# A linear-attention and bilinear-FFN block: the second layer norm of chunks 3 and 4 regrouped through DRAM and transposed in 32x32 blocks

## The chip, the cores and the metric

The kernel runs on one core of one Trainium2 chip. The core has five engines that run their own instruction streams and meet at semaphores: TensorE (PE; its weight loads are listed apart as PEld), VectorE (DVE), ScalarE (ACT), GpSimd (POOL) and SyncE (SP), which here only issues DMAs. The metric is the device time of one execution in microseconds, lower is better; a time shown is the median of several runs.

## What is computed

A transformer block with adaptive layer norm on 2048 tokens of width D = 512: attention without softmax with 32 heads, then a gated FFN of width F = 1376 without a nonlinearity. Everything is float32.

```
mod = (silu(c) @ w_mod).reshape(1, 6, 1, 512)
sa, ca, ga, sb, cb, gb = mod[:, 0] ... mod[:, 5]
h = layernorm(x) * (1 + ca) + sa
x = x + ga * linear_attention(h, wqkv, wo)
h = layernorm(x) * (1 + cb) + sb          # the second layer norm
x = x + gb * (((h @ w_gate) * (h @ w_up)) @ w_down)
```

## The kernel before

**Tiling.** The 2048 tokens are four chunks of four tiles; a tile is 128 tokens (partitions) by 512. The code counts chunks from 0, so "chunks 3 and 4" of the change are `ch` = 2 and 3. Each f32 product is made of three products in a narrower float format: an operand is split into a rounded high part and the rest (`split`, L190: high on ACT at L191, low on DVE or POOL at L192), and high x high, high x low, low x high are summed in PSUM.

**Buffers.** Nearly all tiles come from one pool `tiles` of NB = 99 buffers of 2 KB a partition (L62, `B` L75). PSUM is two pools of four banks, `ps_acc` and `ps_w`. The schedule is manual: each engine executes its instructions in the order in which the Python code issues them. A buffer is handed on when its last reader is done; an engine that writes into it waits for that. All DMAs go through SP's queue in program order.

**The second layer norm** (`Norm`, L212). Per chunk: statistics on DVE; `rstd_of` and `nmr_of`; `xhat(j)` (L238) normalises tile j on ACT, or `xhat_on` (L244) on DVE; `transpose(k)` (L250) turns feature block k (128 features) of the four tiles by four TensorE transposes of 128x128 into one PSUM bank of 128 features x 512 tokens; `modulated` (L263) applies scale `cb[k]` and shift `sb[k]` on ACT from PSUM into an SBUF tile `f` and stores it to DRAM (`kept`). `ln2_turn` (L803) does both for some k. Chunks 0 and 1 (`PLAIN`) are split into high and low there too. Chunks 2 and 3 are loaded back from `kept` later, by `Left.get`.

**The FFN by blocks.** The chunks are taken in pairs, (0, 1) then (2, 3). For one pair and one F tile the gate and up products are made with seven matrix products instead of eight: `Left` (L819) builds from the four quarters a11, a12, a21, a22 of the transposed activations the sums s1 to s4 (DVE) and splits them; `Right` (L874) does the same with the rows of w_gate and w_up (differences on POOL at L888, splits at L899 to L906). For k = 0, 1 (`KH` = 2), a11 is feature block k of the first chunk and a12 block k + 2; a21 and a22 are those of the second chunk. `block` (L938) makes the seven products of one F tile, six matmuls each (`times`, L915), in the banks a, b, c, d:

```
g1: a  = a11 x b11      ACT: copy a to b        p1
g2: d  = s1 x t1        ACT: copy d to u        p5
g3: b += s2 x t2        ACT: copy b to c, to u2 p6
g4: a += a12 x b21                              p2
g5: c += s3 x t3        DVE: p5 = c + u (L979)  p7
g6: d += s4 x b22       DVE: u2 = d + u2 (L983), times a (L948)  p3
g7: c += a22 x t4       DVE: times c (L948)     p4
```

ACT's copies are L925 (called from L956, L962, L966, L968). PE may start g5 only when ACT has copied b to c, and g7 only when DVE has read c at L979. p1 to p7 are points at which other work is put into the engines' streams: p6 scales the w_down tile (L1071), p7 loads the next w_down tile and the weights of block m + 2 and splits those of m + 1, p3 splits the w_down tile, p4 makes the sums of m + 2. At p1, before it, `flush` issues the splits (`kh`, `kl`) of the block before.

**Order around the change.** `ffn` (L1058) is a generator over the blocks m = 0, 1, ... of `steps`; `fill(n)` advances it by n products. The main program (L1105 on) weaves attention of the last chunk, layer norm and FFN together by hand. For `ch` = 2, `ln2_turn` stands beside the attention output of tiles 12 and 13 (L1208, L1212; its PE neighbours are `turn_a` L654, `y_step` L690 and `down` L791). For `ch` = 3 it stands within blocks m = 1 and 2 (L1246 to L1258); there the transposes write to `ps_acc` banks. Then the Left side of the second pair is a list `trickle` of small work items (sums and splits); `some` hands out one at each of the points p1, p5, p6, p3, p4 of blocks m = 2 to 6 (L1077: in m = 2 only at the last three). The split parts go to DRAM (`aside`) and are fetched at blocks 7 and 8. After the first pair's second group, matmuls of the down projection (L1000 to L1002) stand between blocks.

Of the kernel before, what the change touches and what calls it, by code (L numbers as in the profile page):

```python
# [8 lines left out]
F32 = mybir.dt.float32  # L9
F32R = mybir.dt.float32r  # L10
AF = mybir.ActivationFunctionType
# [1 line left out]
AX = mybir.AxisListType  # L13

P = 128
NB = 99
EPS_LN = 1e-5
EPS_PHI = 1e-6
EPS_DEN = 1e-6
# [3 lines left out]
def tile_adaln_block(  # L23
# [12 lines left out]
    nc = tc.nc  # L36
    ctx.enter_context(tc.manual_schedule())
    _, S, D = x.shape
    F = w_gate.shape[1]
    KD = D // P  # L40
    NJ = 4
    CH = NJ * P
    NCH = S // CH
# [10 lines left out]
    wo_v = wo.rearrange("(k p) n -> k p n", p=P)  # L54
    wg_v = w_gate.rearrange("(k p) f -> p k f", p=P)
    wu_v = w_up.rearrange("(k p) f -> p k f", p=P)
    wm_v = w_mod.rearrange("(p k) n -> p k n", k=KD)

    pool = lambda name, bufs, **kw: ctx.enter_context(tc.tile_pool(name=name, bufs=bufs, **kw))
    consts = pool("consts", 1)  # L60
    small = pool("small", 2)
    tiles = pool("tiles", NB)  # L62
    ps_acc = pool("ps_acc", 4, space=bass.MemoryType.PSUM)
# [11 lines left out]
    def B(tag, shape=(P, D), dt=F32):  # L75

        return T(tiles, tag, shape, dt)
# [23 lines left out]
    nc.gpsimd.memset(eps_phi, EPS_PHI)  # L101
    eps_z = consts.tile([P, 1], F32, name="eps_z")
    nc.gpsimd.memset(eps_z, S * EPS_PHI)
    half = consts.tile([P, NJ], F32, name="half")
    nc.gpsimd.memset(half, -0.5)


    def load(src, tag):
        raw = B(tag, (P, *src.shape[1:]))[:src.shape[0]]
        nc.sync.dma_start(raw, src)  # L110
        return raw
# [371 lines left out]
    for i in range(NT):  # L483
        ch, j = divmod(i, NJ)
# [59 lines left out]
    ga, sb, cb = rows[2], cols[3], cols[4]  # L544
# [61 lines left out]
    for k in range(KD):  # L606
        f = B("n")
# [10 lines left out]
    for g in range(KD):  # L618
        a, b = g * P, (g + 1) * P
# [30 lines left out]
    def turn_a(i):  # L650
        tps[i] = turn_bank[0]()
        phi = phq.pop(i)
        for k in range(KD):
            nc.tensor.transpose(tps[i][:, k * P:(k + 1) * P], phi[:, k * P:(k + 1) * P], ident)  # L654
# [64 lines left out]
    norm2 = {}  # L719


    PLAIN = (0, 1)
# [73 lines left out]
    def ln2_xhat(ch):  # L796
        norm2[ch].xhat(0, 1, 2, 3)

    def ln2_nx(ch):
        norm2[ch].nmr_of()  # L800
        ln2_xhat(ch)

    def ln2_turn(ch, *ks, cast=None):  # L803
        norm2[ch].transpose(*ks)
        norm2[ch].modulated(cb, sb, *ks, keep=kept[ch], cast=cast, parts=ch in PLAIN)

    for f in lone:
        load_ffn(f)
    kept = [[tc.dram_tile([P, D], F32, name=f"kept_{ch}_{k}") for k in range(KD)] for ch in range(NCH)]
    for ch in range(NCH):  # L810
        norm2[ch] = Norm(xts[ch])

# [3 lines left out]
    KH = KD // 2  # L816
    SIDE = ("a11", "s1", "s2", "a12", "s3", "a22", "s4")

    class Left:  # L819
# [7 lines left out]
        def get(self, *names):  # L827
            for n in names:
                c, k = self.of[n]
                self.f[n] = load(kept[c][k], "f")  # L830

        def sum(self, *names):
            for n in names:
# [40 lines left out]
    class Right:  # L874


        def __init__(self, f):
            f0, self.n = fts[f]
            self.up, self.low = self.tile("raw"), self.tile("raw")
            for t, kh in ((self.up, 0), (self.low, 1)):  # L880
                for i, v in enumerate((wg_v, wu_v)):
                    nc.sync.dma_start(t[:, i], v[:, kh * KH:(kh + 1) * KH, f0:f0 + self.n])

        def tile(self, tag, dt=F32):
# [139 lines left out]
    steps = [(cs, f) for cs, g in groups for f in g]  # L1024
    rights = {}

    def right_load(n):
        if n < len(steps):
            rights[n] = Right(steps[n][1])

    def right_sums(n, on=None):
        if n < len(steps):
# [14 lines left out]
    trickle = []  # L1047
# [10 lines left out]
    def ffn():  # L1058

        first_side, second_side = side, {}  # L1060
        m = 0
        for g, (cs, fs) in enumerate(groups):
            last = g + 1 == len(groups) or groups[g + 1][0] != cs
            outs, ds = [], []
            A = first_side if cs == (0, 1) else second_side
            for f in fs:
                out = []
                draw = draws.pop(m)

                def scale(d=draw):  # L1070
                    nc.vector.tensor_tensor(d, d, gb[:d.shape[0]], op=ALU.mult)  # L1071

                at = {"p6": [scale],
                      "p7": [lambda: draw_load(m + 1), lambda: right_load(m + 2), lambda: right_split(m + 1)],
                      "p3": [lambda: ds.append(split_raw(draw, low=nc.gpsimd))],
                      "p4": [lambda: right_sums(m + 2)]}
                for point in ("p1", "p5", "p6", "p3", "p4")[2 if m == 2 else 0:]:  # L1077
                    at.setdefault(point, []).append(lambda: some(some_at.get(m, 0)))
                if m + 1 < len(steps) and steps[m + 1][0] != cs:
                    at["p1"].append(lambda: fetch(stash, second_side, "a11", "s1"))  # L1080
                    at["p7"].insert(0, lambda: fetch(stash, second_side, "s2", "a12", "s3"))
# [12 lines left out]
            parts.extend([(ch, i, js, outs, ds, last) for i, (ch, js) in enumerate(zip(cs, jss)) if js] for jss in cut_at)  # L1094
        flush()
        while parts:
            group = parts.pop(0)
            for p in group:
                down_group(*p, by_tile=not parts, end=not parts and p is group[-1])()

    def fill(n):
        for _ in range(n):
            next(work, None)
# [93 lines left out]
    first[0].sum("s1", "s3")  # L1197
    g()
    norm2[2].xhat(2, 3)
    turn_a(12)  # L1200
    take = down(1, (0, 1), parts=((f0, f1), (f2,)))
    turn_h(12)
# [2 lines left out]
    y_banks += [acc_bank(), acc_bank()]  # L1205
    y_seed(12, y_bank)
    first[0].sum("s2", "s4")
    ln2_turn(2, 0, 1)  # L1208
    take()
    den_c(14)  # L1210
    y_step(12, seed=y_bank)
    ln2_turn(2, 2, 3)  # L1212
    take = down(1, (2, 3))
    first[1].sum("s1", "s3", "s2", "s4")
    first[0].split("s1", "s2")
# [26 lines left out]
    norm2[3].rstd_of()  # L1242
    fill(3)
    norm2[3].nmr_of()
    fill(1)
    norm2[3].xhat(0)  # L1246
    norm2[3].xhat_on(nc.vector, 2)
    second = [Left((2, 3), k).aside(stash) for k in range(KH)]
    for x in second:
        x.get("a11", "a12")  # L1250
    fill(2)
    norm2[3].xhat(1)
    fill(1)
    norm2[3].xhat(3)
    fill(2)
    ln2_turn(3, 0, 1)
    fill(1)
    ln2_turn(3, 2, 3)  # L1258
    for x in second:
        x.get("a21", "a22")  # L1260
    for part in zip(*[x.steps() for x in second]):
        for todo_k in part:
            trickle += todo_k
    free[0] = True
    for _ in work:
        pass
# [27 lines left out]
```

## Time and profile before

| | |
|---|---|
| median of 3 runs | 564.64 us (564.09 to 564.94) |
| the profiled execution | 563.91 us |
| its span in the trace | 562.2 us |
| mean granted TensorE clock | 0.999 of full speed |
| PE, DVE, ACT, POOL busy | 556.0, 379.3, 280.7, 192.4 us |
| DMA | 59.34 MB, 106 GB/s on average |

The profile is that of one execution. A line of the timeline gives start and duration in us, engine, source line, operation, output <- inputs with their shape, and how many instructions in a row were joined (x8); in brackets stands the idle time before it and what released it. The duration of a joined row is from the first start to the last end; an instruction's duration contains a part that overlaps the next one's, so the spacing of starts is the pace. A line of a group gives "busy us, mean ns of one | idle before, and who released". A DMA issue line gives count, KB each and the median time from issue to landing. The row of a window gives start:end and its length, then the busy time of PE, PEld, DVE, ACT and POOL with instruction counts, the granted clock, the DMA share and GB/s.

### The profile page before, as it was taken

What the parts mean: (1) busy time and instruction counts of PE and PEld (TensorE: products, weight loads), DVE (VectorE), ACT (ScalarE), POOL (GpSimd) and SP (SyncE); (2) the same over time, 40 slices, a digit from 0 to 9 for tenths busy, and PEclk for the clock granted to TensorE, in tenths of its full rate; (3) what the DMA queues carried; (4) which work ended last, traced back from release to release, by engine and by line L of the source; (5) the groups of instructions that cost most, each with busy time, mean ns of one, the idle gap of its engine ahead of it and who ended that gap; (6) DMA issues with size and microseconds to landing.
All of it is one profiled execution on the core that took longest, in us unless ns stands there. A gap on an engine that the chain in (4) does not pass through costs nothing.

```text
span 562.2 us, 7362 instructions
## 1 busy us (share of the span) xinstructions
PE 556.0 (99%) x2565; PEld 456.9 (81%) x2565; DVE 379.3 (67%) x622; ACT 280.7 (50%) x503; POOL 192.4 (34%) x195
## 2 busy tenths in 40 slices
PE   8999999999999999999999999999999999999997
PEld 6788888888888788878888888887888888888886
DVE  7896968878969876769887877655444444334435
ACT  3695866546557537355885454534333333334120
POOL 2000000000011300001499856556667446446200
PEclk9999999999999999999999999999999999999999
DMA  8900223302302001804409372699337022100004
GB/s 271 386 17 2 75 76 102 124 0 63 93 2 75 1 1 56 244 0 151 132 1 301 111 231 88 202 356 288 113 112 199 7 58 58 56 19 2 0 1 149
DMA packets 50309, 59.34 MB, mean 106 GB/s; under 512 B 6432, under 2 KB 27168, under 8 KB 50272
## 3 DMA queue, kind: packets, MB, share of 16 engines
q1 hardware_dynamic: 50272, 58.87, 32.7%
q8 instruction: 20, 0.33, 0.2%
q14 instruction: 17, 0.14, 0.1%
HBM read 43.12 MB, written 15.73 MB: 105 GB/s over the span
## 4 chain that ended last, share of the span: by engine, by line
PE 92%; issue 2%; POOL 2%; DVE 1%; ACT 1%; DMA 1%; SPq 1%; POOLq 0%
PE bank L920 29%; PE acc L1000 6%; PE acc L1001 6%; PE acc L1002 6%; PE acc L690 6%; PE bank L204 5%; PE bank L206 5%; PE bank L205 5%; PE acc L333 3%; PE acc L332 3%; PE acc L331 3%; PE bank L769 2%; PE bank L767 2%; PE bank L768 2%; PE bank L254 2%
## 5 line engine op out<-in xcount | busy, mean ns | idle before, releaser
L920 PE MATMUL bank<-h,w 128*128 128x512 f32 (+1 forms) x798 | 184.7, 390 | 0.0
L920 PEld LDWEIGHTS bank<-h,w 128*128 128x128 f32 (+1 forms) x798 | 148.3, 186 | 32.7 <-DVE u L979 0.3
L925 ACT ACTIVATE bank<-bank 128x512 f32<-128x512 f32 (+1 forms) x38 | 22.1, 583 | 143.1 <-PE bank L920 143.1
L754 DVE TENSOR_TENSOR x<-acc,x 128x512 f32<-128x512 f32 (+1 forms) x73 | 48.9, 682 | 47.7 <-PE acc L1002 46.9
L906 POOL TENSOR_TENSOR w<-raw,w 128x256 fp32r<-128x256 f32 (+3 forms) x38 | 41.9, 1103 | 101.9 <-ACT w L899 74.7
L1000 PE MATMUL acc<-w,kh 128*128 128x512 f32 (+2 forms) x154 | 59.6, 387 | 0.0
L1001 PE MATMUL acc<-w,kh 128*128 128x512 f32 (+2 forms) x154 | 59.6, 387 | 0.0
L1002 PE MATMUL acc<-w,kl 128*128 128x512 f32 (+2 forms) x154 | 59.5, 386 | 0.0
L192 POOL TENSOR_TENSOR w<-raw,w 128x512 fp32r<-128x512 f32 (+1 forms) x25 | 35.4, 1419 | 54.2 <-ACT w L191 28.4
L232 POOL TENSOR_TENSOR rstd<-ve,half 128x4 f32<-128x4 f32 (+1 forms) x10 | 10.7, 1068 | 122.7 <-DVE ve L231 121.7
L906 POOL TENSOR_TENSOR w<-t,w 128x512 fp32r<-128x512 f32 (+1 forms) x38 | 49.3, 1315 | 0.0
L192 DVE TENSOR_TENSOR kl<-u,kh 128x512 fp32r<-128x512 f32 (+1 forms) x38 | 27.6, 767 | 31.5 <-ACT kh L191 25.8
L204 PE MATMUL bank<-w,h 128*128 128x512 f32 x104 | 40.8, 392 | 0.0
L206 PE MATMUL bank<-w,h 128*128 128x512 f32 x104 | 40.5, 390 | 0.0
L205 PE MATMUL bank<-w,h 128*128 128x512 f32 x104 | 40.5, 389 | 0.0
L690 PE MATMUL acc<-w,xh 128*128 128x512 f32 x120 | 38.1, 399 | 0.0
L1000 PEld LDWEIGHTS acc<-w,kh 128*128 128x128 f32 (+1 forms) x154 | 28.9, 188 | 6.0
L1002 PEld LDWEIGHTS acc<-w,kl 128*128 128x128 f32 (+1 forms) x154 | 28.9, 188 | 6.0
L1001 PEld LDWEIGHTS acc<-w,kh 128*128 128x128 f32 (+1 forms) x154 | 28.9, 188 | 5.9
L979 DVE TENSOR_TENSOR u<-bank,u 128x512 f32<-128x512 f32 (+1 forms) x19 | 13.1, 691 | 29.4 <-PE bank L920 25.9
L241 ACT ACTIVATE n<-x,nmr,rstd 128x512 f32<-128x512 f32 x29 | 22.1, 803 | 16.1 <-DVE nmr L235 14.8
L191 ACT ACTIVATE w<-raw 128x512 fp32r<-128x512 f32 (+2 forms) x44 | 26.4, 619 | 3.0 <-DMA raw<-in_A_wqkv_dram 1.3
(199 smaller groups left out, 1116.0 us busy)
## 6 DMA issues: line engine op xcount, KB each, us to landing
raw<-in_w_mod_dram SPq DMA_DIRECT2D x24, 256.0 KB, 4.6
raw<-in_B_w_down_dram SPq DMA_DIRECT2D x20, 256.0 KB, 3.2
raw<-in_B_w_gate_dram SPq DMA_DIRECT2D x36, 128.0 KB, 3.6
raw<-in_B_w_up_dram SPq DMA_DIRECT2D x36, 128.0 KB, 3.6
x<-in_A_x_dram SPq DMA_DIRECT2D x16, 256.0 KB, 5.4
kept<-f SPq DMA_DIRECT2D x16, 256.0 KB, 2.0
f<-kept SPq DMA_DIRECT2D x16, 256.0 KB, 4.6
side_s<-h SPq DMA_DIRECT2D x16, 256.0 KB, 2.4
```

The source lines that it names most:

```text
L191: nc.scalar.activation(h, src, AF.Copy)
L192: (low or nc.vector).tensor_tensor(l, src, f32(h), op=ALU.subtract)
L204: nc.tensor.matmul(ps, ah, bh, start=i == 0, stop=False)
L205: nc.tensor.matmul(ps, ah, bl, start=False, stop=False)
L206: nc.tensor.matmul(ps, al, bh, start=False, stop=i == n - 1)
L690: nc.tensor.matmul(yps[i], x, y, start=False, stop=k == KD - 1 and x is al, skip_group_check=True)
L754: nc.vector.tensor_tensor(xt[:, a:b], dn[j][:, a:b], xt[:, a:b], op=ALU.add)
L906: sub = lambda out, x, y: (on or nc.gpsimd).tensor_tensor(out, x, f32(y), op=ALU.subtract)
L920: mm = lambda x, y, **kw: nc.tensor.matmul(ps, x[:, k], y, skip_group_check=True, **kw)
L1000: nc.tensor.matmul(ps, hh[:, a:b], dh[:n, c:d], start=i == 0, stop=False)
L1001: nc.tensor.matmul(ps, hh[:, a:b], dl[:n, c:d], start=False, stop=False)
L1002: nc.tensor.matmul(ps, hl[:, a:b], dh[:n, c:d], start=False, stop=i == len(hs) - 1)
```

## The change

For chunks 2 and 3 the 32 TensorE transposes go. Each normalised tile is stored to DRAM in four stores of 32 partitions (`stow`), in such an order that, loaded back as a tile (`unstow`), a partition holds the tokens and the feature quarter that belong together; a VectorE transpose of 128x512 in 32x32 blocks (`flip`) then turns it into one slice of a constant tile `wide` with features on partitions; `flipped` applies scale and shift on ACT from `wide` into a tile `f` that stays in SBUF for `Left.get`. Partition p then holds the features 4p to 4p + 3, so that feature block k is every fourth feature instead of 128 adjoining ones: the scale and shift columns are laid out anew (`by_fours`), and the rows of w_gate and w_up are loaded in that grouping for the second pair (`wg_4`, `wu_4`). NB falls from 99 to 94. `flip` and `flipped` of chunk 2 and both of chunk 3 partly become items of `trickle`, which now has other items in another order, and block m = 2 hands items out at all five points.

```diff
-NB = 99
+NB = 94
+BL = 32
+NQ = P // BL
...
+    wg_4 = w_gate.rearrange("(p k) f -> p k f", p=P)
+    wu_4 = w_up.rearrange("(p k) f -> p k f", p=P)
...
+    wide = consts.tile([P, NJ, D], F32, name="wide")
...
+    def by_fours(col, name):
+        t, v = consts.tile([P, KD], F32, name=name), tc.dram_tile([D], F32, name=name + "_row")
+        nc.sync.dma_start(v.rearrange("(k p) -> p k", p=P), col)
+        nc.sync.dma_start(t, v.rearrange("(p k) -> p k", k=KD))
+        return t
+
+    def stow(ch, *js):
+        for j in js:
+            to = stowed[ch, j] = tc.dram_tile([P, D], F32, name=f"stowed_{ch}_{j}")
+            to = to.rearrange("(q i) (m c) -> m i q c", i=BL, c=P)
+            for m in range(NQ):
+                nc.sync.dma_start(to[m], norm2[ch].n[j][m * BL:(m + 1) * BL].rearrange("i (q c) -> i q c", c=P))
+
+    def unstow(ch):
+        for j in range(NJ):
+            blocks[ch, j] = load(stowed[ch, j], "u")
+
+    def flip(ch, *js):
+        for j in js:
+            nc.vector.transpose(wide[:, j].rearrange("p (m s i) -> p m s i", m=NQ, i=BL),
+                                blocks.pop((ch, j)).rearrange("p (m i s) -> p m s i", m=NQ, i=BL))
+
+    def flipped(ch, *ks):
+        for k in ks:
+            f = B("f")
+            nc.scalar.activation(f.rearrange("p (x i) -> p x i", i=BL),
+                                 wide.rearrange("p j (m s i) -> p (j m) s i", m=NQ, i=BL)[:, :, k],
+                                 AF.Identity, scale=cb4[:, k:k + 1], bias=sb4[:, k:k + 1])
+            blocks[ch, "f", k] = f
...
+    cb4, sb4 = by_fours(cb, "cb4"), by_fours(sb, "sb4")
...
-                self.f[n] = load(kept[c][k], "f")
+                self.f[n] = load(kept[c][k], "f") if c in PLAIN else blocks.pop((c, "f", k))
...
-                for i, v in enumerate((wg_v, wu_v)):
+                for i, v in enumerate((wg_v, wu_v) if plain else (wg_4, wu_4)):
...
-                for point in ("p1", "p5", "p6", "p3", "p4")[2 if m == 2 else 0:]:
+                for point in ("p1", "p5", "p6", "p3", "p4"):
...
     norm2[2].xhat(2, 3)
+    stow(2, 0, 1, 2, 3)
...
-    ln2_turn(2, 0, 1)
     take()
...
-    ln2_turn(2, 2, 3)
...
     norm2[3].nmr_of()
+    unstow(2)
+    for j in range(NJ):
+        fill(1)
+        norm2[3].xhat(j)
+        stow(3, j)
+        flip(2, j)
     fill(1)
-    norm2[3].xhat(0)
-    norm2[3].xhat_on(nc.vector, 2)
     second = [Left((2, 3), k).aside(stash) for k in range(KH)]
-    for x in second:
-        x.get("a11", "a12")
-    fill(2)
-    norm2[3].xhat(1)
-    fill(1)
-    norm2[3].xhat(3)
-    fill(2)
-    ln2_turn(3, 0, 1)
-    fill(1)
-    ln2_turn(3, 2, 3)
-    for x in second:
-        x.get("a21", "a22")
-    for part in zip(*[x.steps() for x in second]):
-        for todo_k in part:
-            trickle += todo_k
+
+    def turned(k, ch, *names):
+        return lambda: (flipped(ch, k, KH + k), second[k].get(*names))
+
+    trickle += [turned(0, 2, "a11", "a12"), lambda: second[0].split("a11"), lambda: second[0].split("a12"),
+                turned(1, 2, "a11", "a12"), lambda: (unstow(3), second[1].split("a11")), lambda: second[1].split("a12"),
+                lambda: flip(3, 0, 1), lambda: flip(3, 2, 3)]
+    for k in range(KH):
+        late = second[k].steps()[1]
+        trickle += [turned(k, 3, "a21", "a22"), lambda a=late: (a[0](), a[1]()), lambda a=late: (a[2](), a[3]()), *late[4:]]
```

More of the change, by code (lines that the diff above doesn't have):

```diff
@@ L801, in ln2_nx @@
         ln2_xhat(ch)
+    def by_fours(col, name):
[23 more added lines that the diff above has]
+            blocks[ch, "f", k] = f
+    stowed, blocks = {}, {}
     def ln2_turn(ch, *ks, cast=None):
@@ L808, in tile_adaln_block @@
         load_ffn(f)
-    kept = [[tc.dram_tile([P, D], F32, name=f"kept_{ch}_{k}") for k in range(KD)] for ch in range(NCH)]
+    kept = [[tc.dram_tile([P, D], F32, name=f"kept_{ch}_{k}") for k in range(KD)] for ch in PLAIN]
+    cb4, sb4 = by_fours(cb, "cb4"), by_fours(sb, "sb4")
     for ch in range(NCH):
@@ L874, in tile_adaln_block, with __init__ @@
     class Right:
-        def __init__(self, f):
+        def __init__(self, f, plain):
             f0, self.n = fts[f]
@@ L1028, in right_load @@
         if n < len(steps):
-            rights[n] = Right(steps[n][1])
+            rights[n] = Right(steps[n][1], steps[n][0][0] in PLAIN)
     def right_sums(n, on=None):
```

## The prediction

> **What bounds the kernel now.** I read the page first: the busy table, then the chain of waits; then engine totals by window, and each engine's timeline around the 32 transposes.
>
> ```profile
> span 562.2 us, 7362 instructions
> PE 556.0 (99%) x2565; PEld 456.9 (81%) x2565; DVE 379.3 (67%) x622; ACT 280.7 (50%) x503; POOL 192.4 (34%) x195
> ...
> PE 92%; issue 2%; POOL 2%; DVE 1%; ACT 1%; DMA 1%; SPq 1%; POOLq 0%
> ```
>
> TensorE works 556.0 of 562.2 us and carries 92% of the chain that ended last. So a microsecond taken off PE is a microsecond of time, unless PE then finds an operand not ready. Any wait newly put on PE is paid in full. The profiled execution took 563.91 us, 1.7 us of it around the span; the median shown is 564.64, 0.73 us above. I work out differences and add them to the median.
>
> ```profile
> 252.65 1.04 PE L254 MATMUL bank<-ident,n 128*128 128x128 f32 x8
> 253.52 0.60 PE L654 MATMUL bank<-ident,h 128*128 128x128 f32 x4
> ...
> 256.74 1.04 PE L254 MATMUL bank<-ident,n 128*128 128x128 f32 x8
> 257.53 0.47 PE L791 MATMUL acc<-w,kh 128*128 128x512 f32 x1
> ...
> 289.30 2.66 PE L920 MATMUL bank<-h,w 128*128 128x512 f32 x11
> 291.80 1.33 PE L254 MATMUL acc<-ident,n 128*128 128x128 f32 x8
> 292.88 1.63 PE L920 MATMUL bank<-h,w 128*128 128x512 f32 x6
> 294.35 1.03 PE L254 MATMUL acc<-ident,n 128*128 128x128 f32 x8
> 295.14 3.21 PE L920 MATMUL bank<-h,w 128*128 128x512 f32 x13
> ...
> 307.48 9.25 PE L920 MATMUL bank<-h,w 128*128 128x512 f32 x40
> ```
>
> PE never pauses here. The last row gives the pace of a 512-column matmul: (9.25 - 0.39)/39 = 0.227 us, 0.39 being one matmul's own length. A group of six takes 1.363 us, a block of seven groups (L938) 9.55 us. If a block starts at s, its fifth group g5 is due at s + 5.45 and its seventh, g7, at s + 8.18.
>
> **Gain: the transposes.** Chunk index 2: 253.52 - 252.65 = 0.87 and 257.53 - 256.74 = 0.79, together 1.66 us. Chunk index 3: from 289.30 to 295.14 pass 5.84 us, in which 17 L920 matmuls need 3.86; the rest, 1.98 us, are transposes. **Sum -3.64 us.** What remains is to find where PE now arrives before its operands.
>
> **What takes their place, and its prices.** Gone too are eight L266 activations out of PSUM and, for chunks 2 and 3, eight kept stores and eight loads of them. New are eight stows of four stores each, eight loads, eight flips on DVE, eight `flipped` on ACT, four tiny constant loads (issued with the first FFN weights, long before their use, which hides them) and a pool five buffers smaller. The normalisation of one tile (L247) moves from DVE to ACT; ACT's blocks hold gaps there, and if they didn't, it would cost at most its 0.80 us (first row). w_gate and w_up rows are grouped otherwise in the same 512-byte pieces: nothing.
>
> ```profile
> L241 ACT ACTIVATE n<-x,nmr,rstd 128x512 f32<-128x512 f32 x29 | 22.1, 803 | 16.1 <-DVE nmr L235 14.8
> ...
> L266 ACT ACTIVATE f<-acc,col,col 128x512 f32<-128x512 f32 x4 | 2.9, 767 | 0.0
> ...
> L274 DVE CAST h<-f 128x512 fp32r<-128x512 f32 x19 | 8.0, 418 | 1.7 <-ACT f L266 1.7
> ...
> kept<-f SPq DMA_DIRECT2D x16, 256.0 KB, 2.0
> f<-kept SPq DMA_DIRECT2D x16, 256.0 KB, 4.6
> ...
> raw<-in_B_w_gate_dram SPq DMA_DIRECT2D x36, 128.0 KB, 3.6
> ```
>
> `flipped` is the L266/L241 activation with a 32-element-run source; two in a row I take at 1.44 us, the pace of paired L266 work. No DVE transpose stands in this trace. Below it is bounded by the CAST, 0.42 us; above by a two-operand operation slowed beside GpSimd, 1.22 us (row at 313.64 below). I take 0.62 us, about the pace from start to start of undisturbed 128x512 f32 operations (252.45 to 253.05 and 311.83 to 312.43, both below: 0.60), because a flip reads one operand; both ends go into the range. [...]
>
> A stow piece is 64 KB in 512-byte pieces. Landing lies between kept's 2.0 and f's 4.6 us; the w_gate loads, also of 512-byte pieces, show 3.6. Chunk 2 is stowed near 247 us and read near 287, so tens of microseconds cover it. For chunk 3, normalised up to about 293 and read by flips near 311, SP has the stores, then the next w_down and w_gate/w_up loads, then the four loads that wait for the stores to land, and behind these the weights of m=4; all fit by about 4 us. I price the DMAs at nothing; if cover fails, see rival D.
>
> **Wait 1, chunk 2's place.**
>
> ```profile
> 252.45 0.68 DVE L583 SCALAR_TENSOR_TENSOR h<-h,den 128x512 f32<-128x512 f32 x1
> 253.05 0.68 DVE L837 TENSOR_TENSOR s<-s,f 128x512 f32<-128x512 f32 x1
> ```
>
> With the first eight transposes gone PE reaches L654 at 252.65, but L654 transposes L583's result, complete at 253.13 plus its hand-over. DVE is busy without a gap before that, so it can't come earlier: **+0.55 us** (0.45 to 0.65).
>
> **Waits 2 and 4, ACT in blocks m=2 and m=5.** g5 writes bank c, which ACT must first have filled (copy(c, b), L966). Ahead of it ACT does, in order: copy(b, a), two splits kh of the block before, item p1, copy to u, item p5.
>
> ```profile
> 292.22 0.57 ACT L925 ACTIVATE bank<-bank 128x512 f32<-128x512 f32 x1
> 292.73 1.13 ACT L191 ACTIVATE kh<-u 128x512 fp32r<-128x512 f32 x2
> ...
> 324.09 0.58 ACT L925 ACTIVATE bank<-bank 128x512 f32<-128x512 f32 x1 [8.86 <-PE bank L920]
> ...
> 327.14 0.60 ACT L925 ACTIVATE bank<-bank 128x512 f32<-128x512 f32 x1
> ...
> 339.07 0.58 ACT L925 ACTIVATE bank<-bank 128x512 f32<-128x512 f32 x1 [6.88 <-PE bank L920]
> ```
>
> m=4 calibrates: copy(b, a) starts 1.62 after s, so g5 is due at 324.09 - 1.62 + 5.45 = 327.92; copy(c, b) ends 327.74 with two splits (1.04 us) as its items. So the items may last about 1.25 us. In the changed order m=2 has two `flipped` and one split, 1.44 + 0.52 = 1.96. There s = 289.30 + 5 x 0.227 = 290.44 (five of the eleven matmuls close m=1) and g5 is due at 295.89. From 292.22: copy 0.5, splits 1.04, two `flipped` 1.44, copy 0.48, split 0.52, copy 0.58: done 296.78. **+0.9 us** (0.3 to 1.4). m=5 has the same three items: from 339.07, 0.5 + 1.04 + 0.52 + 0.48 + 1.44 + 0.58 end at 343.63, due 342.90: **+0.75 us** (0.2 to 1.2). If `flipped` cost 1.0 apiece, both rise by 0.56.
>
> **Wait 3, DVE in m=1 to m=3.** g7 needs bank c read by the L979 addition.
>
> ```profile
> 286.94 0.96 DVE L247 TENSOR_SCALAR n<-x,mv,rstd 128x512 f32<-128x512 f32 x1
> 287.98 0.69 DVE L979 TENSOR_TENSOR u<-bank,u 128x512 f32<-128x512 f32 x1
> ...
> 293.37 2.96 DVE L192 TENSOR_TENSOR kl<-u,kh 128x512 fp32r<-128x512 f32 x2 [1.07 <-ACT kh L191]
> ...
> 299.52 0.69 DVE L979 TENSOR_TENSOR u<-bank,u 128x512 f32<-128x512 f32 x1 [0.20 <-PE bank L920]
> ...
> 310.25 1.66 DVE L192 TENSOR_TENSOR kl<-u,kh 128x512 fp32r<-128x512 f32 x2 [1.88 <-DMA side_a<-h]
> 311.83 0.68 DVE L192 TENSOR_TENSOR h<-f,h 128x512 fp32r<-128x512 f32 x1
> 312.43 0.68 DVE L837 TENSOR_TENSOR s<-f,f 128x512 f32<-128x512 f32 x1
> ...
> 313.64 1.22 DVE L837 TENSOR_TENSOR s<-f,f 128x512 f32<-128x512 f32 x1
> 314.78 0.68 DVE L979 TENSOR_TENSOR u<-bank,u 128x512 f32<-128x512 f32 x1
> ```
>
> In m=1 two flips replace the L247 row: L979 ends 286.94 + 1.24 + 0.69 = 288.87, g7 is due at 290.44 - 1.36 = 289.08: nothing, but 0.95 if a flip takes 1.2. In m=2 the two kl subtractions took 2.96 us beside a busy GpSimd; with g7 1.98 us earlier, at 298.62 plus wait 2, L979 comes about level: **+0.1** (0 to 1.0). In m=3 four flips come ahead of L979 where two L837 sums were. kl and one L192 end at 312.43; two flips to 313.67; L1071 then falls where the L837 row took 1.14 to its successor, to 314.8; two flips to 316.05; L979 to 316.74. g7 is due at 307.48 + 8.18 = 315.66: **+1.1 us** (0.3 to 3.4, by flips of 0.42 or 1.2).
>
> **Wait 5, five tile buffers fewer.** The new constant `wide` takes four, and NB falls by five for the whole kernel.
>
> ```profile
> 104.09 0.60 ACT L295 ACTIVATE phi<-bank 128x512 f32<-128x512 f32 x1 [2.66 <-PE acc L332]
> ...
> 122.26 0.68 DVE L316 TENSOR_TENSOR z<-z,phi 128x512 f32<-128x512 f32 x1
> ...
> 123.69 1.29 POOL L192 TENSOR_TENSOR w<-z,w 128x512 fp32r<-128x512 f32 x1 [23.97 <-ACT w L191]
> ...
> 125.61 0.64 PE L180 MATMUL bank<-w,ones_r 128*128 128x512 f32 x2
> ```
>
> In the k/v phase ACT waits for a buffer already (L295, released by a late PE reader). With 94 the built program hands each buffer on one reader later. Replayed with these durations, ACT falls behind but DVE mostly catches up, and the last z sum (L316) comes some 1.2 us later (my estimate, between 0 and ACT's whole lag of 4). POOL's low part then ends at 123.69 + 1.2 + 1.29 = 126.2; the second row-sum matmul wants it at 125.61 + 0.24 = 125.85: **+0.4 us** (0 to 1.2).
>
> Sum: -3.64 + 0.55 + 0.9 + 0.75 + 0.1 + 1.1 + 0.4 = +0.2, rounded to +0.3 for m=4's sums on DVE (0 to 0.3): **564.9 us**.
>
> **Rivals.** *B, the waits mostly stay away.* Flips run near the CAST's 0.42 us, ACT's copies release PE sooner than my order of them says, and the shorter pool costs nothing. Then only wait 1 and some 0.5 of the others stand: 564.64 - 3.64 + 1.05 = 562.05; with wait 1 alone 561.55. For it: in the 30 us from 278 to 308 DVE idles 5.6 and ACT 9.05, by the window's row (third and fourth busy figure); against it: the gaps are before g5 and g7 already narrow.
>
> ```profile
> 278.00:308.00 30.00, 29.92 (x141) 24.75 (x140) 24.40 (x31) 20.95 (x39) 28.94 (x25) 1.00 0.42 127
> ```
>
> *C, flips slow down beside GpSimd.* POOL is busy 28.94 of those 30 us (last of the five), and DVE rows there stretch from 0.68 to 1.22 and more. If flips do so too, at 1.2 us, m=1 pays 0.95 and m=3 2.3 more: 564.9 + 3.25 = 568.1. It decides from flips of 0.67 us on, where m=1's 0.2 us of slack is used up. Against it: those rows have two SBUF operands, a flip one.
>
> *D, small stores hold up the queue.* SP sends every transfer, each behind the eighth before it. If the sixteen 64 KB stores of chunk 3 land as slowly as f's 4.6 us, two rounds take 9.2 us and m=3's weights come about 5 us later, against 4 of slack: +1, and 565.9. [...]
>
> *E, the transposes were covered anyway.* Then nothing changes, 564.6. Against it: PE has no gap on either side.
>
> **How the numbers follow.** Forecast A 0.40 (its own range 563.6 to 566.2), B 0.28, C 0.25, D 0.05, E 0.02. The measurement tells differences over 0.2%, 1.1 us, from none: bounds 563.5 and 565.8. Faster: 0.05 of A and 0.27 of B, 0.32. Same: 0.22 of A, 0.01 of B and E, 0.25. Slower: 0.13 of A, C and D, 0.43. Range 561.4 (B with wait 1 alone) to 568.5 (C with a little of D).
>
> **What would show it.** Right: PE busy falls by about 3.6 us (near 552) while the span stays; PE waits at L654 near 252 (released by DVE L583), before g5 in m=2 and m=5 (by ACT L925), before g7 in m=3 (by DVE L979), and at L180 near 126 (by POOL L192). B: these waits are absent. C: transposes averaging over 1 us, DVE waits in m=1 as well. D: SP waiting for the stow transfers and PE or POOL for w_gate loads. Wrong altogether: a flip or `flipped` far outside 0.42 to 1.2 us, or a wait of several microseconds elsewhere, for instance late in the kernel, where buffers are handed on too.

## The result, and the profile after

| | before | changed |
|---|---|---|
| median of 6 runs | 564.37 us (563.55 to 565.62) | 568.63 us (567.91 to 569.88) |
| ratio | | 1.0077 (95% interval 1.0059 to 1.0095) |
| span of the profiled execution | 562.2 us | 566.4 us |

The kernel became 4.3 us slower, where 564.9 was forecast, and lies just past the end of the range (568.5). The time is close to rival C's 568.1.

The page of the changed kernel, busy table and chain of waits:

```profile
span 566.4 us, 7342 instructions
PE 554.0 (98%) x2533; PEld 452.6 (80%) x2533; DVE 385.4 (68%) x629; ACT 281.1 (50%) x503; POOL 190.6 (34%) x195
...
PE 85%; DVE 5%; ACT 4%; issue 2%; DMA 2%; POOL 1%; SPq 1%; ACTq 0%; POOLq 0%; DVEq 0%
```

PE's busy time fell by 2.0 us, to 554.0 and not to the 552 that the prediction named as a sign: of a late matmul's wait the trace counts the first 0.16 us, and of a short wait more, as busy (below). PE still carries most of the chain, but DVE and ACT, 1% each before, now have 5% and 4%: work of theirs ends last in places where PE waits. The view of PE's waits names them (who waits, for whom, total us, times, longest):

```profile
PE bank L960 <- DVE u L1019: 3.2, 2, 2.6
...
PE bank L960 <- ACT bank L965: 1.8, 2, 1.2
...
PE bank L659 <- DVE h L588: 0.4, 1, 0.4
```

Before, none of the three was there. (L960, L1019, L965, L659 are L920, L979, L925, L654 of before; further down L988, L1111, L196, L197 are L948, L1071, L191, L192, while L829 is `flip` and L835 `flipped`.) A wait is counted from a matmul's modelled end, 0.39 us after its start, while the pace is 0.227, so each costs 0.16 us more than shown. Shorter waits show only as a wider row. The full loss is read from where the same instruction stands in both kernels, for example the first matmul of the down projections after m=2, 3, 4 and 5, first before, then changed (PE timeline):

```profile
302.04 0.39 PE L1000 MATMUL acc<-w,kh 128*128 128x512 f32 x1
...
317.03 0.39 PE L1000 MATMUL acc<-w,kh 128*128 128x512 f32 x1
...
332.01 0.39 PE L1000 MATMUL acc<-w,kh 128*128 128x512 f32 x1
...
347.13 0.40 PE L1000 MATMUL acc<-w,kh 128*128 128x512 f32 x1
```

```profile
301.82 0.39 PE L1040 MATMUL acc<-w,kh 128*128 128x512 f32 x1
...
319.68 0.39 PE L1040 MATMUL acc<-w,kh 128*128 128x512 f32 x1
...
335.09 0.39 PE L1040 MATMUL acc<-w,kh 128*128 128x512 f32 x1
...
350.99 0.39 PE L1040 MATMUL acc<-w,kh 128*128 128x512 f32 x1
```

The changed kernel is 0.22 us ahead after m=2 and 2.65 behind after m=3. Call such a difference the displacement. Its steps from 124.9 us on (where it is -0.18) to the last down projection (543.38 against 539.31, +4.07), beside the forecast's terms and beside a later experiment:

| step of the displacement, us | forecast | changed | e9_stow_dense |
|---|---|---|---|
| second row sum at 126 (wait 5) | +0.40 | +0.37 | +0.39 |
| chunk 2's place, 252.4 to 257.5 (1.66 less wait 1) | -1.11 | -1.09 | -1.08 |
| m=1 and m=2 (1.98 less m=1, wait 2, L979) | -0.98 | +0.58 | -1.04 |
| m=3 (wait 3) | +1.10 | +2.87 | +0.82 |
| m=4 | +0.1 | +0.43 | +0.42 |
| m=5 (wait 4) | +0.75 | +0.78 | +0.78 |
| the rest, in steps under 0.2 | 0 | +0.31 | +0.32 |
| sum | +0.3 | +4.25 | +0.61 |

Two rows are wrong, m=1 with m=2 and m=3, by 1.56 and 1.77 us. These are the rows with flips. DVE in m=3 (timeline of the changed kernel) shows why:

```profile
309.97 1.29 DVE L197 TENSOR_TENSOR kl<-u,kh 128x512 fp32r<-128x512 f32 x2 [1.82 <-ACT kh L196]
311.18 0.69 DVE L197 TENSOR_TENSOR h<-f,h 128x512 fp32r<-128x512 f32 x1
311.78 2.10 DVE L829 STREAM_TRANSPOSE wide<-u 128x512 f32<-128x512 f32 x2
313.81 1.73 DVE L1111 TENSOR_TENSOR raw<-raw,row 128x512 f32<-128x512 f32 x1
315.47 2.07 DVE L829 STREAM_TRANSPOSE wide<-u 128x512 f32<-128x512 f32 x2
317.48 0.64 DVE L1019 TENSOR_TENSOR u<-bank,u 128x512 f32<-128x512 f32 x1
```

The order is the forecast's, the durations are not. Two flips take from 311.78 to 313.81, 1.02 us each, where 0.62 was taken. The POOL timeline says that GpSimd did not slow the first:

```profile
308.60 0.73 POOL L928 TENSOR_TENSOR t<-raw,t 128x256 f32<-128x256 f32 x1
313.01 0.74 POOL L946 TENSOR_TENSOR w<-raw,w 128x256 fp32r<-128x256 f32 x1 [3.67 <-ACT w L939]
```

POOL stood still for 3.67 us up to 313.01, all through the first flip, and the pair was as long as one beside a busy POOL (2.07 for two at 315.47; the eight flips lie between 1.046 and 1.119 us each). So the price was near rival C's, but its reason, contention, falls. ACT in m=2:

```profile
292.49 0.62 ACT L196 ACTIVATE kh<-u 128x512 fp32r<-128x512 f32 x1
293.61 0.63 ACT L196 ACTIVATE kh<-u 128x512 fp32r<-128x512 f32 x1 [0.49 <-DVE u L988]
294.14 1.51 ACT L835 ACTIVATE f<-wide,sb,cb 128x512 f32<-128x512 f32 x2
295.55 0.57 ACT L965 ACTIVATE u<-bank 128x512 f32<-128x512 f32 x1
296.03 0.62 ACT L196 ACTIVATE h<-f 128x512 fp32r<-128x512 f32 x1
296.55 0.58 ACT L965 ACTIVATE bank<-bank 128x512 f32<-128x512 f32 x1
```

`flipped` costs 0.71 apiece from start to start, as forecast (0.72). But the second kh waited 0.49 for L988, which stood on DVE behind the fourth flip: the dear flip reached ACT too, and PE's wait before g5 became 1.20 + 0.16 us. Before g7 of m=2 PE stood some 0.4 us more behind L1019 (299.59, 0.68 long), where 0.1 was forecast; with cheap flips (e9_stow_dense) that wait is gone.

### The profile page after: what moved, and what is told of

The parts are those of the page before. It is cut to its first block, busy times and chain, and to the rows that moved or that the text cites. A ratio compares the mean times of both kernels' runs of the same rounds, so it can differ in the third digit from the quotient of the medians.

```text
span 566.4 us, 7342 instructions
## 1 busy us (share of the span) xinstructions
PE 554.0 (98%) x2533; PEld 452.6 (80%) x2533; DVE 385.4 (68%) x629; ACT 281.1 (50%) x503; POOL 190.6 (34%) x195
## 4 chain that ended last, share of the span: by engine, by line
PE 85%; DVE 5%; ACT 4%; issue 2%; DMA 2%; POOL 1%; SPq 1%; ACTq 0%; POOLq 0%; DVEq 0%
PE bank L960 26%; PE acc L1040 6%; PE acc L1041 6%; PE acc L1042 6%; PE acc L695 6%; PE bank L211 4%; PE bank L210 4%; PE bank L209 4%; PE acc L337 2%; PE acc L336 2%; PE acc L338 2%; PE bank L772 2%; PE bank L774 2%; PE bank L773 2%; PE bank L259 2%
## 5 line engine op out<-in xcount | busy, mean ns | idle before, releaser
L960 PE MATMUL bank<-h,w 128*128 128x512 f32 (+1 forms) x798 | 186.1, 390 | 5.3 <-DVE u L1019 3.2
L960 PEld LDWEIGHTS bank<-h,w 128*128 128x128 f32 (+1 forms) x798 | 148.0, 186 | 40.3 <-DVE u L1019 5.5
L965 ACT ACTIVATE bank<-bank 128x512 f32<-128x512 f32 (+1 forms) x38 | 22.1, 582 | 140.4 <-PE bank L960 140.3
L197 POOL TENSOR_TENSOR w<-raw,w 128x512 fp32r<-128x512 f32 (+1 forms) x25 | 34.5, 1382 | 54.3 <-ACT w L196 54.3
L197 DVE TENSOR_TENSOR kl<-u,kh 128x512 fp32r<-128x512 f32 (+1 forms) x38 | 26.4, 736 | 29.6 <-ACT kh L196 29.6
L1019 DVE TENSOR_TENSOR u<-bank,u 128x512 f32<-128x512 f32 (+1 forms) x19 | 13.0, 685 | 29.1 <-PE bank L960 21.5
L196 ACT ACTIVATE w<-raw 128x512 fp32r<-128x512 f32 (+2 forms) x44 | 26.3, 619 | 3.1 <-DVE raw L1111 1.1
```

The costliest lines, as they stand in the source:

```text
L196: nc.scalar.activation(h, src, AF.Copy)
L197: (low or nc.vector).tensor_tensor(l, src, f32(h), op=ALU.subtract)
L960: mm = lambda x, y, **kw: nc.tensor.matmul(ps, x[:, k], y, skip_group_check=True, **kw)
```

## The experiments

Times are medians beside the kernel before on the same chip (564.06 to 564.25 us). At 124.9 us the profiled executions already stand between 0.6 us ahead of the kernel before and 1.3 behind it (those of e1, e3, e6 and e8, 0.9 to 1.3 behind, have a granted clock of 0.50 for 3.4 us near 16 us); displacements are counted from there.

**What does a flip cost, and why?** Two kernels, each with one edit.

e2_flip_dense: the activation reads by fours, the flip adjoining elements.

```diff
+                    x = x.rearrange("p (q i s) -> p q s i", i=BL, s=NQ)
+                    n = n.rearrange("p (q s i) -> p q s i", i=BL, s=NQ)
-            nc.vector.transpose(wide[:, j].rearrange("p (m s i) -> p m s i", m=NQ, i=BL),
-                                blocks.pop((ch, j)).rearrange("p (m i s) -> p m s i", m=NQ, i=BL))
+            nc.vector.transpose(wide[:, j], blocks.pop((ch, j)))
```

> The changed kernel, but the normalising activation of chunks 2 and 3 reads its row by fours, so that the flip reads 512 adjoining elements instead of every fourth; the same values come out. Flips took 1.03 us from start to start in the changed kernel. Theory A (a 32x32 transpose of f32 costs that by itself): flips stay at 1.0 to 1.05 us and the time at 568 to 569. Theory B (the read of every fourth element costs it): flips at about 0.6, the wait before the seventh product in m=1 (0.76 us) goes and that in m=3 falls from 2.7 to about 1.1, time near 566.

e3_copy_strided:

```diff
-            nc.vector.transpose(wide[:, j].rearrange("p (m s i) -> p m s i", m=NQ, i=BL),
+            nc.vector.tensor_copy(wide[:, j].rearrange("p (m s i) -> p m s i", m=NQ, i=BL),
```

> The changed kernel with a plain copy in place of each flip, with the same read of every fourth element and the same output; the blocks are not transposed. Theory A (the transpose itself is dear): copies of 0.4 to 0.65 us, the wait in m=1 gone, that in m=3 at 1.1 us or less, time 565 to 566.3. Theory B (the strided read is dear): copies near 1 us and time near 568.5. Theory C (DVE work beside GpSimd is slowed, whatever it is): copies of 1 us where POOL works and shorter elsewhere.

Measured: 569.57 us, ratio 1.0083 (1.0067 to 1.0099), and 566.22 us, 1.0034 (1.0021 to 1.0048). The group of the flips (busy us, mean ns) in the changed kernel, then in e2_flip_dense, and last the copies of m=3 in e3_copy_strided with the row that ended GpSimd's pause there (timeline):

```profile
L829 DVE STREAM_TRANSPOSE wide<-u 128x512 f32<-128x512 f32 x8 | 8.5, 1088 | 0.0
```

```profile
L834 DVE STREAM_TRANSPOSE wide<-u 128x512 f32<-128x512 f32 x8 | 5.3, 690 | 0.0
```

```profile
314.08 1.15 DVE L829 COPY wide<-u 128x512 f32<-128x512 f32 x2
...
315.75 2.81 DVE L829 COPY wide<-u 128x512 f32<-128x512 f32 x2
```

```profile
315.30 1.13 POOL L946 TENSOR_TENSOR w<-raw,w 128x256 fp32r<-128x256 f32 x1 [3.69 <-ACT w L939]
```

A flip of adjoining elements takes 0.69 us (662 to 705 ns for all that were run in e2_flip_dense and e9_stow_dense, 0.60 from start to start), one of every fourth 1.09. So theory A falls, and theory B is right for the flip: the stride costs it 0.4 us. The strided copies took 0.61 and 0.62 us while POOL stood still (314.08); beside a working POOL one took 0.60 and the five others 1.17 to 1.73. That is theory C, for the copy and not for the flip. Whether a copy pays for the stride as well is not shown, since no kernel here has a copy of adjoining elements to compare (the nearest row, the CAST, took 0.42). Nor does the trace explain the 566.2 us: the profiled execution took 568.91, 2.7 above the median, with waits before g7 in m=1 (0.85) and m=3 (1.33).

The time of e2_flip_dense did not fall, which theory B had wrong: the stride had only moved. Two normalising activations of chunk 2, changed kernel and then e2_flip_dense:

```profile
246.83 1.52 ACT L246 ACTIVATE n<-x,nmr,rstd 128x512 f32<-128x512 f32 x2 [3.17 <-DVE nmr L240]
```

```profile
247.07 2.54 ACT L251 ACTIVATE n<-x,nmr,rstd 128x512 f32<-128x512 f32 x2 [3.17 <-DVE nmr L241]
```

0.5 us more per tile on ACT; PE then waited 2.27 us at the place of L654, ran at a lower clock after it (last section), and waited 2.8 us in all for ACT's copies in m=2 and m=5. The waits for L1019 in m=1 and m=3 were gone.

**Is the forecast right with a cheap flip?** e5_rows_dense lets the weight rows follow the flip's order, with loads in four parts:

```diff
+                    for q in range(NQ):
+                        nc.sync.dma_start(t[q * BL:(q + 1) * BL, i], v[q, :, kh * KH:(kh + 1) * KH, f0:f0 + self.n])
```

> The changed kernel with flips that read adjoining elements, and no other engine pays for it: the features are grouped as the flip then leaves them (32 adjoining ones in a block) by the loads of w_gate, w_up and of the scale and shift columns, each in four parts of 32 partitions. Theory (the read of every fourth element is what made the flip dear, and the flips' surplus of 0.43 us is paid on PE in m=1 to m=3): flips at 0.60 us, the wait of 0.76 us in m=1 gone, that in m=3 from 2.74 to about 1.0, a little less in m=2 and m=4, time 565.3 to 565.9. The waits on ACT in m=2 and m=5 stay near 0.9 and 0.75. Rival (most of the loss is elsewhere): 567.5 or more. Second rival (four times as many weight loads hold up SP): PE or POOL waits for w_gate loads from m=6 on.

Measured: 575.11 us, 1.0194 (1.0170 to 1.0218). The theory held up to m=5, and a relative of the second rival came after it: at the down projection of m=5 PE stood 0.2 us ahead of the kernel before (0.6 ahead at 124.9 us), without a wait in m=1 and with 0.56 in m=3. Then, in m=8, it waited 6.2 us, not for w_gate but for side_s loads:

```profile
PE bank L964 <- DMA h<-side_s: 6.2, 2, 4.6
```

SP issued the last of them from 391.1 us on, behind sixteen weight loads that took it from 382.2 to 391.0, and PE ran at a granted clock of 0.50 from 393.5 to 403.7, worth another 5 us.

e9_stow_dense gets the cheap flip without more loads. The activation reads runs of 32, so that a partition's features lie 128 apart and weights and columns stay as before:

```diff
+                    x = x.rearrange("p (s q i) -> p q s i", i=BL, s=NQ)
+                    n = n.rearrange("p (q s i) -> p q s i", i=BL, s=NQ)
...
+            nc.vector.transpose(wide[:, j], blocks.pop((ch, j)))
...
-                                 AF.Identity, scale=cb4[:, k:k + 1], bias=sb4[:, k:k + 1])
+                                 AF.Identity, scale=cb[:, k:k + 1], bias=sb[:, k:k + 1])
```

> The changed kernel with flips of adjoining elements, this time without more loads: the normalising activation reads its row in runs of 32 in another order, so that a partition's four features lie 128 apart as in the kernel before, and w_gate, w_up, cb and sb are used as there. With the weight loads cut in four, PE stood 0.3 us behind the kernel before at m=5 (start-up taken off), where the changed kernel stands 4.0 behind; it lost 10 us only later, to late side_s loads. Theory (the fourfold loads made that later loss; the dear flip is what the forecast lacked): flips at 0.60 us, no wait in m=1, 0.9 to 1.0 us before g5 in m=2 (ACT), 0.5 to 0.8 before g7 in m=3 (DVE), 0.76 before g5 in m=5 (ACT), time 564.3 to 565.3. Rival (normalising in runs costs ACT as much as reading by fours did, 0.5 us a tile): waits at L659 and in m=2 of 1 us and more each, time over 567. Second rival (late side_s loads come with any version of the new path): over 570.

Measured: 565.05 us against 564.25, ratio 1.0018 (1.0008 to 1.0027). The flips and PE's waits:

```profile
L824 DVE STREAM_TRANSPOSE wide<-u 128x512 f32<-128x512 f32 x8 | 5.3, 684 | 0.0
```

```profile
PE bank L953 <- ACT bank L958: 1.4, 2, 0.8
...
PE bank L953 <- DVE u L1012: 0.6, 1, 0.6
PE bank L661 <- DVE h L590: 0.4, 1, 0.4
```

They are the waits of the forecast, at its places: ACT before g5 in m=2 (0.81) and m=5 (0.60), DVE before g7 in m=3 (0.56), L654's place (0.39). The table's last column follows the forecast within 0.35 us in every row. The whole is 0.8 us above the kernel before (0.5 to 1.5 by the interval), where the forecast had 0.3. The edit also changes the order in which ACT reads (its normalisation stays at 0.80 us a tile) and goes back to the old layout of weights and columns, but the two rows that were wrong are right again, and the time goes from 568.6 to 565.1.

**What does the shorter pool cost?** e1_pool94: NB = 94 in the kernel before, `wide` reserved and unused.

> The kernel before with 94 tile buffers in place of 99 and the constant tile wide reserved but unused; nothing else. Theory (five buffers fewer cost PE a short wait in the k/v phase, as wait 5 of the prediction says): the matmuls after the second row sum start 0.3 to 0.5 us later than before from about 126 us on, and the whole is 0.4 to 0.6 us longer, near 564.9. Rival (the pool size is harmless, the 0.36 us that the changed kernel shows there comes from something else): no shift at 126 us, time as before. Second rival (the shorter pool is what costs the changed kernel its 4 us): 566 or more.

Measured: 564.29 us, 0.9996 (0.9987 to 1.0006). No effect on the time can be told; the interval ends at +0.3 us. The two row-sum matmuls show the wait (PE timeline, e1_pool94; before, the row read 0.64):

```profile
126.63 1.02 PE L181 MATMUL bank<-w,ones_r 128*128 128x512 f32 x2
```

0.38 us longer, as in every kernel here with 94 buffers and in none with 99. Wait 5 is in the traces and as large as forecast; in the time it is at or below what can be resolved.

**What were the transposes worth?** e4_no_turn leaves them out of the kernel before and puts nothing in their place; e8_no_turn_no_mod leaves out chunk 3's scale and shift as well.

```diff
-                for j in range(NJ):
-                    nc.tensor.transpose(ps[:, j * P:(j + 1) * P], self.n[j][:, k * P:(k + 1) * P], ident)
-                self.ps[k] = ps
+                self.ps[k] = ps if self.turns else self.n[k]
```

> The kernel before without the 32 transposes of chunks 2 and 3: the scale-and-shift activations read the normalised tiles directly, so their features stay on the free axis. Theory: PE gives back the 3.64 us less a wait of about 0.5 us at L654 for the den product on DVE: 561.1 to 561.6. Rival (the transposes were covered, or other waits fill the gap at once): 563 or more.

> The kernel before without the 32 transposes, as in the earlier run, and without the four scale-and-shift activations of chunk 3 on ACT either: the kept tiles are the normalised ones. With the activations left in, PE waited 1.82 us before g5 of m=2 for ACT, and then ran for 4 us at a granted clock of 0.57. Theory (chunk 3's transposes covered the time that ACT needed there; with ACT relieved by 2.8 us both the wait and the low clock go): 560.8 to 561.6. Rival (something else holds PE in m=2): 563 or more, with another releaser.

Measured: 564.20 us, 0.9986 (0.9972 to 1.0001), and 563.63 us, 0.9986 (0.9976 to 0.9995). Both theories missed, by 2.0 us and more; the rivals fit. PE in m=2 of e4_no_turn, and its window (the last figures are clock, DMA share, GB/s):

```profile
297.02 5.99 PE L921 MATMUL bank<-h,w 128*128 128x512 f32 x18 [1.82 <-ACT bank L926]
```

```profile
297.00:301.00 4.00, 3.98 (x10) 3.13 (x11) 1.39 (x2) 3.95 (x9) 4.00 (x5) 0.57 0.84 266
```

Without chunk 3's sixteen transposes g5 comes 1.98 us earlier and waits that long for ACT, whose four activations now end last; and in the 4 us after the wait the granted clock is 0.57, which costs another 1.7 us. That is the traced run: three of its ten runs took 562.2 to 562.7 us at a mean clock of 0.998 or 0.999, the seven others 563.5 to 565.3 at 0.997 or less, so the clock seems to have held in some. In e8_no_turn_no_mod ACT is relieved, and PE waits for DVE's L979 instead, 0.70 us in m=2 and 1.07 in m=3. So in this order of items chunk 3's transposes stood where PE would else have waited, and only chunk 2's, 1.1 us net of wait 1, could be had.

**Can the waits be ordered away?** e6_late_items moves most items behind g7 (up to m=7); e7_dense_late does that with e5_rows_dense's cheap flips. Their core:

```diff
+    trickle[2, "p4"] = [lambda: unstow(3), lambda: turned(0, 2, "a11", "a12"), lambda: second[0].split("a11", "a12")]
+    trickle[3, "p4"] = [lambda: turned(1, 2, "a11", "a12"), lambda: second[1].split("a11", "a12")]
+    trickle[4, "p3"] = [lambda: flip(3, 0, 1)]
+    trickle[4, "p4"] = [lambda: flip(3, 2, 3), lambda: turned(0, 3, "a21", "a22")]
...
+    trickle[7, "p5"] = [lambda: second[1].split("s4")]
```

> The changed kernel with its own dear flips, and only the order of the work items changed: in m=1 one flip stands before L1019 in place of two; flipped, flips of chunk 3, sums and splits stand at p3 and p4, behind the last product of a block, where ACT and DVE wait for the down projection, and none in m=2 and m=3 before g7. Theory (the losses are operands late for g5 and g7 in m=1 to m=5, not the amount of work): all these waits go, and of the 3.64 us gained only the wait at L659 (0.5) and that at 126 us (0.36) are given back: 561.3 to 562.3. Rival (the work itself is too much for DVE or ACT, or the split parts come too late to DRAM for block m=8): 564 or more, with waits in m=4 to m=8.

> Both edits of the two kernels before this one together. Theory: with the items late the flip's price hardly counts, so the time is that of the late items alone within 0.5 us, 561 to 562.3. Rival (the flip's price counts wherever it stands): 1 us or more below the kernel with late items and dear flips.

Measured: 576.14 us, 1.0203 (1.0177 to 1.0229), and 580.52 us, 1.0278 (1.0261 to 1.0295). Up to m=5 the theory held: at the down projection of m=5 e6_late_items stands 2.09 us ahead of the kernel before after 0.91 behind at 124.9 us, so 3.0 us gained, without a wait in m=1 to m=5. Then the postponed work struck: 3.16 us before g7 of m=6 for DVE's L1019, and in m=8 some 3 us for side_s and side_a loads, late because their stores were, with a granted clock of 0.50 from 394.9 to 401.7 us (0.991 in the mean of the execution, 0.999 in the kernel before). e7_dense_late has the same wait in m=6 and, with the fourfold weight loads as well, 8.4 us for side_s loads; it came out 4.4 us above e6_late_items, which neither its theory nor its rival had.

e10_dense_order ends all items in m=6 and gives each block what it can bear, with e9_stow_dense's flips; e11_order has that order with the changed kernel's dear flips.

```diff
+    trickle[2, "p1"] = [lambda: turned(0, 2, "a11")]
+    trickle[2, "p5"] = [lambda: x.split("a11")]
+    trickle[2, "p6"] = [lambda: turned(0, 2, "a12")]
...
+    trickle[3, "p3"] = [lambda: flip(3, 0, 1)]
+    trickle[3, "p4"] = [lambda: flip(3, 2, 3), lambda: turned(0, 3, "a21"), lambda: turned(0, 3, "a22")]
...
+    trickle[6, "p3"] = [lambda: y.split("s4")]
```

> The kernel before this one with the work items laid out by what each block can bear: at most one flipped and one split before g5, chunk 3's flips at p3 and p4 of m=3, the rest at p3 and p4, and all items done by p3 of m=6 as in the changed kernel. Theory (the waits on ACT in m=2 and m=5 and on DVE in m=3 are a matter of order): they go, only those at L659 (0.5) and 126 us (0.36) stay: 561.2 to 562.3, faster than both kernels. Rival (work moved behind g7 comes back as waits of the next block or as late side_s loads): 564 or more.

> The changed kernel with its dear flips and the order of items of the kernel above. In m=1 two flips still stand before L1019. Theory: the wait of 0.76 us in m=1 and some 0.4 in m=2 stay, those in m=3 to m=5 go: 562.2 to 563.3. Rival (the dear flips cost their time wherever they stand): 565 or more.

Measured: 563.14 us, 0.9982 (0.9972 to 0.9993), and 563.79 us, 0.9994 (0.9980 to 1.0008). Both are slower than expected, but e10_dense_order is faster than both kernels, by about 1.1 us than before (0.4 to 1.6) and 5.5 than the change. Its waits:

```profile
PE bank L953 <- ACT bank L958: 0.4, 1, 0.4
PE bank L661 <- DVE h L590: 0.4, 1, 0.4
PE bank L953 <- DMA h<-side_a: 0.2, 1, 0.2
PE bank L953 <- DMA h<-side_s: 0.2, 1, 0.2
```

Of 1.45 us gained up to m=7, the DMA waits of m=8 took back all and more (displacement -1.45 to +0.28) in the profiled execution, which took 564.20, 1.1 above the median. In that of e11_order, 0.6 us ahead at m=7, m=8 took nothing. The two medians are 0.65 apart, and their intervals overlap: in this order of items the dear flips cost some 0.7 us, which can't be told from nothing, where in the changed kernel's order they cost 3.5. e12_fetch_early writes the first of those loads at an earlier place of the program:

```diff
-                    at["p1"].append(lambda: fetch(stash, second_side, "a11", "s1"))
+                if m + 2 < len(steps) and steps[m + 1][0] == cs and steps[m + 2][0] != cs:
+                    at["p4"].append(lambda: fetch(stash, second_side, "a11", "s1"))
```

> The dense flips and the new order of items again, with one more edit: the first eight loads of the split parts (a11, s1) are issued at p4 of m=6 instead of p1 of m=7. With the new order PE was 1.45 us ahead of the kernel before at the down projection of m=7 and 0.3 behind at that of m=8: inside m=8 it waited for side_s and side_a loads while the DMA engines were busy without a gap from 360 to 390 us, and at 0.14 to 0.5 of their time from 350 to 358. Theory (the gain is lost there to transfers that start too late): those waits go, 561.2 to 562.2. Rival (that stretch is bound by its bytes, or the buffers come free no earlier): 562.8 to 563.5, with the same waits.

Measured: 563.45 us, 0.9987 (0.9975 to 0.9999), the rival's time. But the edit moved nothing: no other transfer stands between the two places, SP's transfers come in the same order in both traces, and the loads began at 363.4 us against 363.2. So the run repeats e10_dense_order (563.14) and does not test the theory. Ahead of the loads SP had six side_s stores, waiting for their splits, from 347.7 to 358.2 us (347.5 to 358.0 in e10_dense_order). Whether loads issued from another queue would save the stretch was not tried.

## Why the prediction was wrong

The step that failed is the price of a flip, "I take 0.62 us ... because a flip reads one operand". It measured 1.02 from start to start, because the change's flip reads every fourth element of its row; one that reads adjoining elements takes 0.60, as the estimate had it. The upper bound of 1.22 held, but for another reason than the one given, so the choice between the bounds, made by the number of operands, went the wrong way. The price told because of where the flips stood, ahead of L1019 and of ACT's kh: with the items in another order (e11_order) the same dear flips left the time at 563.8. The row that would have warned is missing from the trace before: no DVE instruction there transposes, and I did not weigh the access pattern of the flip's input, which stands in the diff.

Point by point. *PE's time taken off*: 1.66 us is seen whole at chunk 2's place; e4_no_turn shows that the other 1.98 could not be had by leaving the transposes out alone, which the forecast allowed for in wait 2. *Wait 1*: right (0.55 forecast; 1.66 - 1.09 = 0.57). *Wait 2*: its place and releaser right; 1.36 against 0.9, the surplus being kh held up 0.49 by a flip; with cheap flips 0.97. The L979 term of m=2 was 0.1 and measured about 0.4. *Wait 4*: right, 0.76 against 0.75. *Wait 3*: place right; m=3 was priced 1.1 and cost 2.87, of which four flips at 0.4 more make 1.6. In m=1 nothing was forecast, and 0.60 + 0.16 came, 0.95 being the working's own figure for flips of 1.2. *Wait 5*: right, 0.37 against 0.4; POOL's low part came 1.1 us later against PE in e1_pool94, where 1.2 was estimated. *m=4's sums*: 0.43 against 0 to 0.3, with cheap flips too.

The rivals: C's place, point (flips over 0.67) and time were what happened; its mechanism fell, since flips run as long when POOL stands still. That its time is so near is in part luck: it took 1.2 us a flip and 0.95 + 2.3 us for m=1 and m=3, where 0.76 + 1.77 came, and what it did not have (0.8 us more than forecast in m=2, 0.3 in m=4) made up for it. D did not occur in the change (stows landed in 1.8 us, median), but a relative of it did in e5_rows_dense, where weight loads four times as many and a quarter as large held up later loads, and PE waited 6.2 us. E holds for chunk 3's half of the transposes, in the order of the kernel before. B did not happen.

What stays open: why the strided read makes the transpose dearer, and whether a copy pays for it too.

## What to carry to other kernels

Price an instruction by its operation and its access pattern together, and when the trace has no row for that pair, keep both bounds alive as forecasts of their own; here one stride was worth 3.5 us of a change of 4.3, and some 0.7 with the work items in another order. Moving work off a busy engine gains only where the other engines' operands are already there (3.64 us of transposes left out of PE gave a ratio of 0.9986, 0.9972 to 1.0001, in e4_no_turn): list, for each freed place, the next producer and its slack, as the forecast's waits did. An inconvenient layout is best absorbed where it costs nothing: here in an activation that reads in runs of 32 (0.80 us a tile, as before), not in the flip (0.4 us more each), not by fours on ACT (0.5 us more a tile), and not in four times as many loads (6.2 us of waits in m=8 of e5_rows_dense).

## What the runs showed of the hardware that was not expected

Around some waits of PE its granted clock fell: to 0.57 over the 4 us after a wait of 1.82 us (e4_no_turn), to 0.68 over 254 to 258 us after 2.27 us (e2_flip_dense, where the four transposes at 255.71 took 1.12 us against 0.60 before), to 0.50 from 393.5 to 403.7 us beside waits of 4.6 and 1.6 us on loads (e5_rows_dense), to 0.50 over 362 to 366 us beside one of 3.2 us (e7_dense_late); but it was 1.00 over 318 to 322 us after 2.58 us (changed kernel) and 1.00 over 362 to 366 us after 3.16 us in e6_late_items. In e4_no_turn wait and clock together come to some 3.5 us (1.82, and 0.43 of 4 us). From the windows' figures I estimate that the stretches at 0.50 lasted 3.4 us (e4_no_turn, and near 16 us in e1_pool94 and e6_late_items), 6.8 us (e7_dense_late) and 10.2 us (e5_rows_dense): one, two and three times the same length. The length of the wait does not decide by itself: 1.82 us came with the low clock, 2.58 us did not, and of two waits of 3.2 us one did. What decides stays open.

DVE's transpose was not slowed by GpSimd: two flips of the changed kernel took 2.11 us at 286.15, where POOL was busy for all 7.00 us from 286 to 293, and 2.10 us at 311.78, where it stood still up to 313.01 (all eight 1,046 to 1,119 ns). A plain copy of the strided row took 0.61 us without GpSimd and, beside it, 0.60 once and else 1.17 to 1.73.
